# Attention and feed-forward on one core: the opening's order on all five engines as lists of numbers

## The chip, the cores and the metric

The kernel runs on one core of a Trainium2 chip. The metric is the device time of one execution in microseconds (us). TensorE (PE), VectorE (DVE), ScalarE (ACT), GpSimd (POOL) and SyncE (SP, which here issues nearly all DMAs) each work through a list of their own, in order, and wait for one another by semaphores.

## The reference, cut to what matters

Eight batches, eight heads of 64 columns, 512 local and 32 global tokens. Local tokens attend to a band of 32 positions on both sides and to the global tokens; global tokens attend to everything. What comes out, 8 x 544 rows of 512, goes through a feed-forward layer with a residual:

```python
xn = (x - mu) / np.sqrt(var + 1e-06) * g_ln
ch = np.maximum(xn @ w_ch1, 0.0) @ w_ch2      # 512 -> 2048 -> 512
return (x + ch).astype(np.float32)
```

## The kernel before, in words

**Chunks and units.** The local rows are cut into eight chunks of 512 rows (one batch, two halves of 256 rows), the global rows form a ninth. Attention is done in units: one pair of heads of one half. A unit has `score` (32 PE matmuls), four `lowest` (DVE), four `exp` (ACT), `turn` (4 PE transposes) and `turned` (ACT copy), `sums` (32 PE matmuls), `total` (POOL), `inverse` and `scale` (DVE). The first chunk has units 0 to 7, four for each half. After a half's four units come `stats`, `join`, `widen` (DVE), `root` (POOL) and `apply` (DVE, one of the four on ACT), which norm the rows, and then the turning of the normed rows: `turn_x` on PE, `high_x` on ACT and `low_x` on DVE, which split a float32 into two terms for PE.

**Feed-forward.** Each chunk runs through 16 weight blocks f: `first` (three groups of four 128x512 matmuls into `ph`), `high` (ACT, `hh`, L694) and `low` (DVE, `hl`, L698), and `second` (three matmuls for each of four row tiles). The next block's `first` reuses the one bank of `ph`, so it waits for the `hl` before it. Below, FFN0 and FFN1 are the `first` of blocks 0 and 1 in the first chunk, and hh0, hl0, hl1, ... the two terms of a block's result.

**Weights.** Each block is loaded once in a packed form (`raw`, two DMAs, .0 for the first matrix and .1 for the second) and unpacked during the first chunk, in two parts of seven steps: `size`, `third` and `high` on ACT (L293, L296, L315), `bound`, `place`, `sign` and `low` on DVE (L300, L303, L309, L319). Four places hold raw blocks, so block 4 can be loaded when block 0's `sign` steps are done, and so on.

**Later units.** While a chunk is in its feed-forward, PE visits the next chunk's units two at a time: a *visit* scores two units and sums the two before them. Units 8 to 15 are visited in the first chunk.

**The planner.** No order is left to the framework. `begin_plan` describes every operation to `Plan.op` (engine, cost, key, what it comes after), numbered here from 0 as they are described, and `Plan.emit` plays the engines in a model: among an engine's operations that can start soonest (within `PATIENCE`) it takes the smallest key, emits it and adds its cost to the engine's time. The model also has the DMA wire, and PE's code, fetched in pages of 256 words while PE works (`PAGE`, `FETCH`). In PE's idle time it emits dummy matmuls (`none`, L810).

Of the kernel before, what the change touches and what calls it, by code (L numbers as in the profile page):

```python
# [75 lines left out]
IN_FLIGHT = 8  # L76
STORING = 6


class Plan:  # L80


# [6 lines left out]
    def op(self, engine, cost, key, run, *after, behind=None, late=0.0, size=0.0, words=8):  # L89
        o = Operation(engine, cost, key, run, after, behind, late, size)  # L90
        o.words = words
        self.waiting[engine].append(o)
        self.count += 1
        return o

    def emit(self):
# [11 lines left out]
        wire, landed, paused = FIRST_BYTE, [], False  # L108
        words, fetched = 0, 0.0
        while self.count:  # L110
# [12 lines left out]
            o = can[e].pop(n)[1]  # L123
            self.count -= 1
            o.end = t + o.cost * (COLD[1] if e == "PE" and t < COLD[0] else 1.0)
            if e == "PE":
                spare = SPARE * (COLD[1] if t < COLD[0] else 1.0)
                idle = max(free[e], AWAKE)
                for _ in range(int((t - idle - MARGIN) / spare) if t < FULL else 0):
                    words += 2 * self.spare(idle)  # L130
                for n in range(words, words + o.words):
                    if n % PAGE == PAGE_AT and t < FULL:
                        now = t + o.cost * (n - words) / o.words
                        if n > PAGE:
# [25 lines left out]
class Operation:  # L160
    def __init__(self, engine, cost, key, run, after, behind, late, size):
        self.engine, self.cost, self.key, self.run = engine, cost, key, run
        self.after = flat(after)
        self.behind, self.late, self.size, self.end = behind, late, size, None

    def lands(self):
        return self.end + self.late + LATENCY

    def ready(self):
        t = self.behind.end if self.behind else 0.0  # L170
        for a in self.after:
            same = a.engine == self.engine and not a.size
            t = max(t, a.end if same else a.end + a.late + LATENCY)
        return t

@with_exitstack
def attention_ffn_kernel(
# [185 lines left out]

    xtags = cycle(["x0", "x1", "x2"])

    def new_x():
        return fpool.tile([P, 2, DM], F32, name="x", tag=next(xtags))

# [417 lines left out]
    def begin_plan(plan):  # L786
# [45 lines left out]
        for n, u in enumerate(us):  # L832
# [8 lines left out]
            for c in range(4):  # L841
# [11 lines left out]
            turned[n] = op(  # L853
                *(("DVE", 0.69) if n in ON_DVE else ("ACT", 0.57)), key + 0.4,
                lambda u=u, n=n: u.turned(n in ON_DVE), turn[n], sums.get(n - 2)
# [14 lines left out]
            def stats(u=u, it=it, hp=hp, j=0):  # L870
                if hp == j == 0:
                    it["norm"] = Norm(u.x, range(2), HP)
                it["norm"].stats(j, hp)
# [6 lines left out]
            if hp < HP - 1:  # L880
# [6 lines left out]
            join = [  # L887
                op("DVE", 0.17, key, lambda it=it, j=j: it["norm"].join(j), it["stats"])
                for j in range(2)
# [4 lines left out]
            for j in range(2):  # L894
                on_act = 2 * half + j in APPLY_ACT

                def apply_to(it=it, j=j, half=half, on_act=on_act):
                    if "to" not in it:
                        it["to"] = new_x() if half else wpool.tile([P, 2, DM], F32, name="x", tag="w4")
# [4 lines left out]
                apply.append(op(  # L904
                    *(("ACT", 0.81) if on_act else ("DVE", 0.55)), key, apply_to, root,
                    it["shift"] if on_act else [],
# [18 lines left out]
            def split_in(k2, it=it, half=half, key=key):  # L925
                for kt in (2 * k2, 2 * k2 + 1):
# [10 lines left out]
                    it["high"].append(op("ACT", 0.38, key + 0.2, high_half, it[k2, "t"], g,  # L937
                                         it["high"][-1:]))
                    it["low"].append(op("DVE", 0.41, key + 0.3, low_half, it["high"][kt]))
# [8 lines left out]
        xl = half_of[1]["low"]  # L948
        xh = half_of[1]["high"]

# [4 lines left out]
        for f in range(NF):  # L955
# [17 lines left out]
            for part, c in enumerate(  # L973
# [3 lines left out]
                key += W2_LATE * part  # L977
                size = op("ACT", 1.13 if wide else 0.6, key, lambda s=s, c=c: s.size(c), raws[f][part if not wide else 1],
                          before)
                before = size  # L980
                third = op("ACT", 1.13 if wide else 0.6, key + 0.1, lambda s=s, c=c: s.third(c), size)
                on, cost = ("POOL", 1.15 if wide else 0.65) if f in ON_POOL else ("DVE", 0.69 if wide else 0.36)
                bound = op(on, cost, key + 0.2, lambda s=s, c=c: s.bound(c), size)
                place = op("DVE", 1.22 if wide else 0.63, key + 0.3, lambda s=s, c=c: s.place(c), bound, third)
                sign[f].append(op("DVE", 1.22 if wide else 0.63, key + 0.4, lambda s=s, c=c: s.sign(c), place))
                high[f].append(op("ACT", 1.04 if wide else 0.56, key + 0.5, lambda s=s, c=c: s.high(c), sign[f][-1]))
                on, cost = ("POOL", 2.3 if wide else 1.2) if f in ON_POOL else ("DVE", 1.22 if wide else 0.63)
                low[f].append(op(on, cost, key + 0.6, lambda s=s, c=c: s.low(c), high[f][-1]))


# [23 lines left out]
        def visit(key, us, prev, nxt):  # L1014
# [31 lines left out]
            for j, u in enumerate(us):  # L1046
# [18 lines left out]
                t = op("POOL", 0.23, key + 0.3, lambda u=u: u.total(), exps)  # L1065
                inverse_of[u] = op("DVE", 0.17, key + 1.0, lambda u=u: u.inverse(), t)
                if not locals_:
# [6 lines left out]
                    for k in range(16):  # L1074
                        turned_of[u].append(
                            op("DVE", 0.31, key + 2, lambda u=u, k=k: u.transposes(*divmod(k, 4)),
                               turned_of[u][1:])
# [7 lines left out]
                else:  # L1085
                    o = []
                    for k in range(16):
                        o.append(op("DVE", 0.31, key + SLACK, lambda u=u, k=k: u.transposes(*divmod(k, 4)),
                                    exps, o[-1:], v))
# [6 lines left out]
            for u in prev:  # L1096
                banks[2].append(op("DVE", 0.42, key + 0.1, lambda u=u: u.scale(), v, inverse_of[u]))
                if u.at[1] == HP - 1:
# [4 lines left out]
        def finish(u, key, scales):  # L1103
# [17 lines left out]
            for j in js:  # L1121
                st.append(op("DVE", 0.69, key, lambda j=j: stats(j), scales, st[-1:]))
            join = [op("DVE", 0.17, key, lambda j=j: it["norm"].join(j), st) for j in js]
            widen = op("DVE", 0.14, key, lambda: it["norm"].widen(), join)
# [46 lines left out]
        for c, chunk in enumerate(chunks):  # L1171
# [29 lines left out]
            for f in range(NF + 1):  # L1201
                key = nominal(c, f)
                if f < NF:
# [26 lines left out]
                    if 2 * f in beside:  # L1230
                        beside[2 * f].behind = end
                    hh[c, f] = op("ACT", 0.59 if wide else 0.38, key - URGENT, lambda f=f, box=box: box[0].high(f),
                                  end, second.get((c, f - 2, nt - 1)))
                    hl[c, f] = op("DVE", 0.66 if wide else 0.39, key - URGENT, lambda f=f, box=box: box[0].low(f),
                                  hh[c, f])
# [179 lines left out]
```

## Time and profile before

| | us |
|---|---|
| median of 3 runs | 908.24 (905.89 to 909.13) |
| the profiled execution, whole | 908.04 |
| its span, first to last instruction | 906.3 |
| PE busy in the span | 890.3 |
| DVE busy | 692.0 |
| ACT busy | 311.5 |
| first feed-forward matmul starts | 39.96 |
| start from which PE has no gap until the end | 45.13 |

A time in the rows is counted from the span's first instruction. A timeline line gives the start, the duration (of a group: from the first to the last), engine, line, operation, tile and, in brackets, the idle time of the engine before it and what ended that. `pv` is what `sums` writes, `sc` what `score` writes, `tp` what `turn` writes, `t` what `turn_x` writes, `x` what `scale` and `apply` write. "issue" as a releaser means that the engine waited for nothing that the profile shows.

### The profile page before, as it was taken

What the parts mean: (1) busy time and instruction counts of PE and PEld (TensorE: products, weight loads), DVE (VectorE), ACT (ScalarE), POOL (GpSimd) and SP (SyncE); (2) the same over time, 40 slices, a digit from 0 to 9 for tenths busy, and PEclk for the clock granted to TensorE, in tenths of its full rate; (3) what the DMA queues carried; (4) which work ended last, traced back from release to release, by engine and by line L of the source; (5) the groups of instructions that cost most, each with busy time, mean ns of one, the idle gap of its engine ahead of it and who ended that gap; (6) DMA issues with size and microseconds to landing.
All of it is one profiled execution on the core that took longest, in us unless ns stands there. A gap on an engine that the chain in (4) does not pass through costs nothing.

```text
span 906.3 us, 21438 instructions
## 1 busy us (share of the span) xinstructions
PE 890.3 (98%) x8523; PEld 709.3 (78%) x8523; DVE 692.0 (76%) x2432; ACT 311.5 (34%) x881; POOL 39.8 (4%) x133
## 2 busy tenths in 40 slices
PE   6899999999999999999999999999999999999997
PEld 4488878888788888878888887888888877777896
DVE  4999998798878888788878896888876266766411
ACT  6799863223223223323323222322323122222211
POOL 4101000000000000000000000000000000000000
PEclk9999999999999999999999999999999999999999
DMA  9787654324124313324332403332331435455200
GB/s 352 278 314 248 227 172 146 100 80 148 37 93 141 111 70 125 102 77 148 105 99 99 148 3 122 108 120 100 125 102 53 155 123 216 156 180 204 67 17 24
DMA packets 42868, 119.88 MB, mean 132 GB/s; under 512 B 5136, under 2 KB 7184, under 8 KB 40720
## 3 DMA queue, kind: packets, MB, share of 16 engines
q1 hardware_dynamic: 42576, 118.25, 37.2%
q8 instruction: 67, 1.10, 0.5%
q14 instruction: 33, 0.27, 0.1%
q10 hardware_dynamic: 192, 0.26, 0.1%
HBM read 100.67 MB, written 17.83 MB: 131 GB/s over the span
## 4 chain that ended last, share of the span: by engine, by line
PE 94%; DVE 0%; issue 0%
PE ph L685 42%; PE acc L710 42%; PE sc L405 3%; PE pv L460 3%; PE pv L594 1%; PE sc L519 1%; PE t L645 0%; PE tp L441 0%; PE tp L567 0%; PE pv L530 0%; DVE tmp L303 0%; DVE ob L722 0%; DVE hl L698 0%
## 5 line engine op out<-in xcount | busy, mean ns | idle before, releaser
L710 PE MATMUL acc<-w,hh 128*128 128x512 f32 x1088 | 342.3, 396 | 0.0
L685 PE MATMUL ph<-xh,w 128*128 128x512 f32 (+1 forms) x1216 | 308.5, 380 | 1.2 <-DVE hl L698 1.0
L685 PEld LDWEIGHTS ph<-xh,w 128*128 128x128 f32 x1216 | 215.7, 188 | 49.4 <-DVE hl L698 1.7
L710 PEld LDWEIGHTS acc<-w,hh 128*128 128x128 f32 x1088 | 205.3, 189 | 47.3
L694 ACT ACTIVATE hh<-ph 128x512 fp32r<-128x512 f32 (+1 forms) x144 | 82.5, 573 | 429.9 <-PE ph L685 400.2
L710 PE MATMUL acc<-w,hl 128*128 128x512 f32 x544 | 218.5, 402 | 0.0
L452 DVE STREAM_TRANSPOSE pt<-p 32x128 f32<-32x128 f32 x768 | 206.1, 289 | 9.4 <-ACT p L429 1.0
L698 DVE SCALAR_TENSOR_TENSOR hl<-ph,hh 128x512 fp32r<-128x512 f32 (+1 forms) x144 | 95.2, 661 | 123.9 <-ACT hh L694 123.1
L685 PE MATMUL ph<-xl,w 128*128 128x512 f32 x512 | 141.2, 397 | 0.0
L429 ACT ACTIVATE p<-p,mn 128x128 f32<-128x128 f32 x256 | 99.6, 392 | 91.2 <-DVE mn L417 91.2
L710 PEld LDWEIGHTS acc<-w,hl 128*128 128x128 f32 x544 | 102.2, 188 | 23.2
L685 PEld LDWEIGHTS ph<-xl,w 128*128 128x128 f32 x512 | 95.8, 188 | 23.6
L653 DVE STREAM_TRANSPOSE tmp<-x 32x128 f32<-32x128 f32 x320 | 96.7, 302 | 4.8
L417 DVE CUSTOM_DVE_ANT_0 p<-sc,mask 128x128 f32<-128x128 f32 x256 | 59.2, 284 | 22.7 <-PE sc L405 20.9
L429 ACT ACTIVATION_READ_ACCUMULATOR p<-p,mn 128x1 f32 x256 | 48.4, 189 | 0.0
L472 POOL TENSOR_SCALAR ri<-sm 128x4 f32<-128x4 f32 x64 | 16.7, 262 | 628.8 <-ACT p L429 627.3
L577 DVE STREAM_TRANSPOSE gpt<-gp 32x128 f32<-32x128 f32 x128 | 38.6, 302 | 2.0
L479 DVE TENSOR_TENSOR x<-pv,ri 128x256 f32<-128x256 f32 x64 | 24.5, 419 | 13.4 <-PE pv L460 13.4
L405 PEld LDWEIGHTS sc<-u_e 64*32 64x32 f32 x1792 | 24.9, 106 | 10.2 <-issue 9.5
L405 PE MATMUL sc<-u_e 64*32 64x128 f32 x1792 | 32.4, 274 | 0.0
L460 PE MATMUL pv<-u_v,pt 128*32 128x64 f32 x1792 | 30.8, 221 | 0.0
L460 PEld LDWEIGHTS pv<-u_v,pt 128*32 128x32 f32 x1792 | 26.3, 110 | 5.7 <-issue 5.7
(71 smaller groups left out, 505.1 us busy)
## 6 DMA issues: line engine op xcount, KB each, us to landing
u_v<-in_ev SPq DMA_DIRECT2D x56, 512.0 KB, 4.8
u_e<-in_eq SPq DMA_DIRECT2D x56, 336.0 KB, 6.3
raw<-in_wd SPq DMA_DIRECT2D x32, 512.0 KB, 7.0
gk<-in_gk SPq DMA_DIRECT2D x8, 1152.0 KB, 6.6
xs<-x SPq DMA_DIRECT2D x32, 256.0 KB, 6.0
ob<-xs SPq DMA_DIRECT2D x32, 256.0 KB, 5.1
out<-ob SPq DMA_DIRECT2D x32, 256.0 KB, 3.5
gv<-in_gv SPq DMA_DIRECT2D x8, 1024.0 KB, 4.9
```

Source lines behind the costliest of these rows:

```text
L405: nc.tensor.matmul(sc[h][gp, qb * P:(qb + 1) * P], self.e[hd, w * WIN:(w + 1) * WIN], self.e[hd, k0 * WIN:(k0 + 4) * WIN], start=True, sto ...
L417: nc.vector.tensor_tensor_reduce(out=self.p[:, c], in0=self.sc[h][:, qb * P:(qb + 1) * P], in1=masks[self.at[2], qb], scale=-QSCALE, scala ...
L429: nc.scalar.activation(self.p[:, c], self.p[:, c], AF.Exp, bias=self.mn[:, c:c + 1], scale=-1.0, accum_out=self.sm[:, c:c + 1],)
L452: nc.vector.transpose(out=self.pt[rp, :, gp], in_=self.p[gp, :, rp])
L460: nc.tensor.matmul(pv[gp, qb * P + h * D:qb * P + h * D + D], self.pt[:, 2 * h + qb, gp], self.v[:, 4 * qb + g, h * D:(h + 1) * D], start= ...
L479: nc.vector.tensor_tensor(self.x[:, :, hp * P:(hp + 1) * P].rearrange("p q (h d) -> p q h d", h=2), self.pv[:, :256].rearrange("p (q h d) ...
L577: nc.vector.transpose(out=self.pt[rp, 0, :, ip], in_=p[ip, :, r])
L653: nc.vector.transpose(out=dst[rp, 2 * half:2 * half + 2, :, i], in_=src[ip, :, k:k + 2, r])
L685: nc.tensor.matmul(self.ph[f][:, :self.n], w[:, kt, :], xx[kt][:, :self.n], start=begins and kt == 0, stop=ends and kt == KT - 1,)
L694: nc.scalar.activation(hh[:, :self.n], self.ph[f][:, :self.n], AF.Relu)
L698: nc.vector.scalar_tensor_tensor(hl[:, :self.n], self.ph[f][:, :self.n], 0.0, f32(hh[:, :self.n]), ALU.max, ALU.subtract,)
L710: nc.tensor.matmul(self.acc[t], a[:, ts], w, start=(f == 0 and i == 0), stop=(f == NF - 1 and i == 2),)
```

## The change

Until its list is used up, an engine takes the operation whose number its list gives next, and no key counts; then the keys take over again. The lists hold the first chunk and some operations of the second: 26 numbers for POOL, 91 for SP, 174 for PE, 227 for ACT, 358 for DVE.

```diff
+        order = {}
+        for e, text in ORDER.items():
...
             for e, ops in can.items():
+                if order[e]:
+                    ops = [(t, o) if o.number == order[e][-1] else (1e9, o) for t, o in ops]
+                    if all(t == 1e9 for t, _ in ops):
+                        continue
                 if not ops:
...
             o = can[e].pop(n)[1]
+            if order[e]:
+                order[e].pop()
```

The stretch of the lists that matters here, in the names above (s unit n as n; W f.p is part p of weight block f; h0, h1 the two halves of the rows):

```
PE   score 0 1 2, turn0, score3, turn1, score4, sums0, turn2, score5, sums1, turn3, score6, sums2,
     turn4, sums3, score7, turn5, sums4, turn6, sums5, turn7, sums6, turn_x h0 (two), sums7,
     turn_x h0 (two), turn_x h1 (four), FFN0, visit 0, FFN1, second of block 0, ...
DVE  ... scale3, three stats, join, lowest7.0, join, widen, lowest7.1, lowest7.2, scale4, lowest7.3,
     stats, W0.1 place, shift, apply0 h0, inverse5, scale5, three stats, inverse7, W0.1 sign,
     inverse6, scale6, W1.0 bound, two stats, low_x h0, scale7, two stats, two joins, widen,
     low_x h0, W1.0 place, W0.0 low, apply h1 (two), low_x h0 (two), W1.0 sign, low_x h1 (four),
     W0.1 low, W1.1 bound, place, sign, W1.0 low, hl0, W1.1 low, ...
ACT  ... exp7.0, turned5, exp7.3, exp7.1, exp7.2, turned6, apply1 h0, W1.0 size, turned7, high_x h0,
     W1.0 third, high_x h0, W1.1 size, W0.0 high, W0.1 high, high_x h0 (two), high_x h1 (four),
     W1.1 third, W1.0 high, W2.0 size, W2.0 third, W2.1 size, hh0, W1.1 high, ..., hh1, ...,
     hh3, W6.0 size, W6.1 size, exp, W6.1 third, exp, exp, W5.0 high, exp, hh4, ...
SP   eq of units 0 1 2 4, raw0.0, eq3, eq5, ev0, eq6, ev2, ev1, raw0.1, raw1.0, ev3, g, eq7, ev4, ev5,
     ev6, raw1.1, raw2.0, ev7, raw2.1, raw3.0, raw3.1, eq8, raw4.0, raw4.1, eq9, eq11, eq10, a store,
     raw5.0, ev8, raw5.1, a store, ev9, ev10, raw6.0, a store, raw6.1, eq13, raw7.0, ...
```

(`eq` and `ev` are the two loads of a unit, scores' and sums' operands.) Besides the lists, the model's costs are set anew (for example 0.36 with a drain of 0.09 for `bound`, 1.22 to 1.14 for a whole `place`, 0.17 to 0.1 for `inverse`, 0.66 to 0.605 for `hl`, 0.31 to 0.275 for a 32x32 transpose), and these hold for all chunks:

```diff
-            inverse[n] = op("DVE", 0.17, key + 0.6, lambda u=u: u.inverse(), total[n])
-            scale[n] = op("DVE", 0.42, key + 0.6, lambda u=u: u.scale(), sums[n], inverse[n])
+            inverse[n] = op("DVE", 0.1, key + 0.6, lambda u=u: u.inverse(), total[n])
+            scale[n] = op("DVE", 0.34, key + 0.6, lambda u=u: u.scale(), sums[n], inverse[n])
+            inverse[n].drain = scale[n].drain = DRAIN
...
-                    hl[c, f] = op("DVE", 0.66 if wide else 0.39, key - URGENT, lambda f=f, box=box: box[0].low(f),
+                    hl[c, f] = op("DVE", 0.605 if wide else 0.34, key - URGENT, lambda f=f, box=box: box[0].low(f),
```

And some dependencies are now written down so that any order keeps them: `high_x` of h1 comes after that of h0, FFN0 after `low_x` of both halves, the second chunk's first `scale` after the last reading of the row tile that it overwrites (`x_read`), and the row tile for h1's normed rows is named ("x2") where it was the next in a cycle. No operation is added or taken away, but the number of dummy matmuls follows the model's idle time.

## Rows read from the trace of the kernel before

**Rows 1.** The chain of waits that ended last, in order of time: start, duration, what. One block's `second`, twelve matmuls as in a `first`.
```profile
48.20 2.81 PE acc L710 x12
```

**Rows 2.** Busy time of each engine in two stretches, with granted clock, DMA share and GB/s.
```profile
0.00:45.13 45.13, 33.91 (x656) 21.09 (x656) 30.54 (x133) 31.77 (x100) 11.76 (x52) 0.92 0.85 315
45.13:900.00 854.87, 854.87 (x7863) 687.29 (x7864) 660.05 (x2298) 279.69 (x781) 28.04 (x81) 1.00 0.35 123
```

**Rows 3.** Waits of PE in the whole span: who waited for whom, us in total, times, longest.
```profile
PE pv L460 <- issue: 4.8, 3, 2.3
...
PE pv L460 <- ACT pt L446: 1.3, 1, 1.3
...
PE ph L685 <- DVE hl L698: 1.0, 1, 1.0
```

**Rows 4.** PE's timeline where the two waits for "issue" end and where as many instructions again have gone by; then the busy time of each engine (PE, PEld, DVE, ACT, POOL, with their instructions) between those points, with PE's granted clock, the DMA share and GB/s.
```profile
14.87 0.53 PE L460 MATMUL pv<-u,pt 128*32 128x64 f32 x19 [2.30 <-issue]
...
20.90 1.07 PE L460 MATMUL pv<-u,pt 128*32 128x64 f32 x28 [2.27 <-issue]
...
26.03 1.17 PE L460 MATMUL pv<-u,pt 128*32 128x64 f32 x32
...
14.86:20.89 6.03, 3.75 (x127) 2.66 (x127) 3.70 (x25) 4.44 (x20) 0.44 (x2) 0.95 1.03 412
20.89:26.95 6.06, 6.05 (x132) 4.67 (x131) 3.61 (x18) 2.64 (x8) 0.94 (x2) 0.50 1.02 412
```

**Rows 5.** Busy time of each engine in the microsecond in which PE's clock is back, columns as in rows 4.
```profile
27.00:28.00 1.00, 0.79 (x25) 0.46 (x22) 0.71 (x3) 1.00 (x5) 0.00 (x0) 0.97 1.02 418
```

**Rows 6.** PE's timeline from the last unit's turn to the end of the last gap.
```profile
28.64 0.72 PE L441 MATMUL tp<-ident,p 128*128 128x128 f32 x4
...
32.16 0.65 PE L460 MATMUL pv<-u,pt 128*32 128x64 f32 x32 [1.29 <-ACT pt L446]
...
37.19 1.11 PE L645 MATMUL t<-ident,x 128*128 128x128 f32 x8
...
39.96 1.18 PE L685 MATMUL ph<-xh,w 128*128 128x512 f32 x4
...
42.94 1.16 PE L405 MATMUL sc<-u_e 64*32 64x128 f32 x64
45.13 1.21 PE L685 MATMUL ph<-xh,w 128*128 128x512 f32 x4 [1.04 <-DVE hl L698]
```

**Rows 7.** DVE's timeline: the last `lowest` of the opening, the end of unit 7 and the second half's norm, the last `low_x`, and the steps before hl0. The last line is from DVE's groups by line and shape up to 45.13 us: busy time, mean ns of one | idle time before them.
```profile
28.11 0.27 DVE L417 CUSTOM_DVE_ANT_0 p<-sc,mask 128x128 f32<-128x128 f32 x1
...
33.52 0.42 DVE L479 TENSOR_TENSOR x<-pv,ri 128x256 f32<-128x256 f32 x1
33.98 0.49 DVE L331 BATCH_NORM_STATS2 st<-x 128x6 f32<-128x128 f32 x2
34.38 0.38 DVE L334 BATCH_NORM_AGGREGATE mv<-st 128x2 f32<-128x24 f32 x2
...
36.59 1.00 DVE L356 TENSOR_SCALAR x<-x,mv,rs 128x512 f32<-128x512 f32 x2
...
39.31 1.65 DVE L663 SCALAR_TENSOR_TENSOR xl<-t,g_sb,xh 128x256 fp32r<-128x256 f32 x4
...
41.93 0.69 DVE L303 SCALAR_TENSOR_TENSOR tmp<-tmp,raw 128x512 int32<-128x512 int32 x1
42.66 0.69 DVE L309 SCALAR_TENSOR_TENSOR tmp<-raw,tmp 128x512 int32<-128x512 int32 x1
43.27 0.42 DVE L300 TENSOR_SCALAR tmp<-tmp 128x512 f32<-128x512 f32 x1
43.78 0.70 DVE L303 SCALAR_TENSOR_TENSOR tmp<-tmp,raw 128x512 int32<-128x512 int32 x1
44.39 0.69 DVE L698 SCALAR_TENSOR_TENSOR hl<-ph,hh 128x512 fp32r<-128x512 f32 x1
...
L417 DVE CUSTOM_DVE_ANT_0 p<-sc,mask 128x128 f32<-128x128 f32 x32 | 7.5, 282 | 6.9 <-PE sc L405 5.4 <-ACT tmp L293 0.7 <-POOL mask L251 0.5
```

**Rows 8.** ACT's timeline: the opening's last `exp` and what follows it, the copy of unit 7's turn, the last `high_x`, and hh0.
```profile
28.49 0.39 ACT L429 ACTIVATE p<-p,mn 128x128 f32<-128x128 f32 x1
...
28.88 0.67 ACT L293 ACTIVATE tmp<-raw 128x512 f32<-128x512 f32 x1
29.45 0.66 ACT L296 ACTIVATE raw<-raw 128x512 int32<-128x512 uint16 x1
...
31.53 0.58 ACT L446 COPY pt<-tp 128x512 f32<-128x512 f32 x1
...
38.12 1.57 ACT L659 ACTIVATE xh<-t,g_sb 128x256 fp32r<-128x256 f32 x4 [1.91 <-PE t L645]
...
43.04 0.60 ACT L694 ACTIVATE hh<-ph 128x512 fp32r<-128x512 f32 x1 [0.60 <-PE ph L685]
```

**Rows 9.** POOL's timeline: the second half's `root`.
```profile
35.05 1.09 POOL L341 TENSOR_TENSOR rs<-rs,neg_half 128x2 f32<-128x2 f32 x1 [5.44 <-DVE rs L337]
```

**Rows 10.** SP's issues of blocks 6 and 7 and of the next unit's operands; then the landing times of the raw tiles issued from 45 to 75 us.
```profile
48.61 9.39 SPq L264 DMA_DIRECT2D raw<-in_wd  x4
58.52 0.80 SPq L264 DMA_DIRECT2D u_v<-in_ev  x2
...
DMA to landing us min/median/max: 4.3/6.2/9.0
```

More of the change, by code (lines that the diff above doesn't have):

```diff
@@ L1 @@
 from contextlib import ExitStack
-from itertools import cycle
+from itertools import chain as run_on, cycle
 import concourse.bass as bass
@@ L91, in op @@
         o.words = words
+        o.number = self.count
         self.waiting[engine].append(o)
@@ L109, in emit @@
         words, fetched = 0, 0.0
+        order = {}
+        for e, text in ORDER.items():
+            order[e] = []
+            for run in text.split():
+                a, _, b = run.partition("-")
+                order[e] += range(int(a), int(b or a) + 1)
+            order[e].reverse()
         while self.count:
@@ L164, in __init__ @@
         self.behind, self.late, self.size, self.end = behind, late, size, None
+        self.drain = 0.0
     def lands(self):
@@ L172, in ready @@
             same = a.engine == self.engine and not a.size
-            t = max(t, a.end if same else a.end + a.late + LATENCY)
+            t = max(t, a.end + a.drain if same else a.end + a.late + LATENCY)
         return t
@@ L362, in att, with new_x @@
         return ps_a.tile([P, 512], F32, name=name, tag=f"att{k}")
-    xtags = cycle(["x0", "x1", "x2"])
-    def new_x():
-        return fpool.tile([P, 2, DM], F32, name="x", tag=next(xtags))
+    xtags = run_on(["x0", "x1"], cycle(["x0", "x1", "x2"]))
+    def new_x(tag=None):
+        return fpool.tile([P, 2, DM], F32, name="x", tag=tag or next(xtags))
     class Local:
@@ L853, in begin_plan @@
             turned[n] = op(
-                *(("DVE", 0.69) if n in ON_DVE else ("ACT", 0.57)), key + 0.4,
+                *(("DVE", 0.69) if n in ON_DVE else ("ACT", 0.48)), key + 0.4,
                 lambda u=u, n=n: u.turned(n in ON_DVE), turn[n], sums.get(n - 2)
@@ L870, in stats @@
             def stats(u=u, it=it, hp=hp, j=0):
-                if hp == j == 0:
+                if "norm" not in it:
                     it["norm"] = Norm(u.x, range(2), HP)
@@ L887, in begin_plan @@
             join = [
-                op("DVE", 0.17, key, lambda it=it, j=j: it["norm"].join(j), it["stats"])
+                op("DVE", 0.1, key, lambda it=it, j=j: it["norm"].join(j), it["stats"])
                 for j in range(2)
@@ L898, in apply_to @@
                     if "to" not in it:
-                        it["to"] = new_x() if half else wpool.tile([P, 2, DM], F32, name="x", tag="w4")
+                        it["to"] = new_x("x2") if half else wpool.tile([P, 2, DM], F32, name="x", tag="w4")
                     (it["norm"].apply if on_act else it["norm"].apply_to)(j, it["to"])
@@ L904, in begin_plan @@
                 apply.append(op(
-                    *(("ACT", 0.81) if on_act else ("DVE", 0.55)), key, apply_to, root,
+                    *(("ACT", 0.72) if on_act else ("DVE", 0.46)), key, apply_to, root,
                     it["shift"] if on_act else [],
@@ L935, in low_half @@
                         low_x(it[kt], *(a[:, cols] for a in xt[kt]), kt)
-                    it["high"].append(op("ACT", 0.38, key + 0.2, high_half, it[k2, "t"], g,
-                                         it["high"][-1:]))
-                    it["low"].append(op("DVE", 0.41, key + 0.3, low_half, it["high"][kt]))
+                    it["high"].append(op("ACT", 0.36, key + 0.2, high_half, it[k2, "t"], g,
+                                         it["high"][-1:], half_of[0]["high"][kt:kt + 1] if half else []))
+                    it["low"].append(op("DVE", 0.395, key + 0.3, low_half, it["high"][kt]))
             steps = [(k2, j) for k2 in range(2) for j in range(2)]
@@ L947, in begin_plan @@
                     split_in(k2)
-        xl = half_of[1]["low"]
-        xh = half_of[1]["high"]
+        xl = half_of[0]["low"] + half_of[1]["low"]
+        xh = half_of[0]["high"] + half_of[1]["high"]
         step = 6.7
@@ L977, in begin_plan @@
                 key += W2_LATE * part
-                size = op("ACT", 1.13 if wide else 0.6, key, lambda s=s, c=c: s.size(c), raws[f][part if not wide else 1],
+                size = op("ACT", 1.11 if wide else 0.575, key, lambda s=s, c=c: s.size(c), raws[f][part if not wide else 1],
                           before)
                 before = size
-                third = op("ACT", 1.13 if wide else 0.6, key + 0.1, lambda s=s, c=c: s.third(c), size)
-                on, cost = ("POOL", 1.15 if wide else 0.65) if f in ON_POOL else ("DVE", 0.69 if wide else 0.36)
+                third = op("ACT", 1.11 if wide else 0.575, key + 0.1, lambda s=s, c=c: s.third(c), size)
+                on, cost = ("POOL", 1.15 if wide else 0.65) if f in ON_POOL else ("DVE", 0.64 if wide else 0.36)
                 bound = op(on, cost, key + 0.2, lambda s=s, c=c: s.bound(c), size)
[L984 to L987, printed above, removed]
+                bound.drain = DRAIN
+                place = op("DVE", 1.14 if wide else 0.605, key + 0.3, lambda s=s, c=c: s.place(c), bound, third)
+                place.drain = DRAIN
+                sign[f].append(op("DVE", 1.14 if wide else 0.605, key + 0.4, lambda s=s, c=c: s.sign(c), place))
+                high[f].append(op("ACT", 1.0 if wide else 0.53, key + 0.5, lambda s=s, c=c: s.high(c), sign[f][-1]))
+                on, cost = ("POOL", 2.3 if wide else 1.2) if f in ON_POOL else ("DVE", 1.14 if wide else 0.605)
                 low[f].append(op(on, cost, key + 0.6, lambda s=s, c=c: s.low(c), high[f][-1]))
+        x_read = [half_of[k]["apply"] + half_of[k]["stores"] for k in range(2)] + [half_of[1]["turn"]]
         free = [[turned[n0 - 2]], [turned[n0 - 1]], lowest[n0 - 1]]
@@ L1065, in visit @@
                 t = op("POOL", 0.23, key + 0.3, lambda u=u: u.total(), exps)
-                inverse_of[u] = op("DVE", 0.17, key + 1.0, lambda u=u: u.inverse(), t)
+                inverse_of[u] = op("DVE", 0.1, key + 1.0, lambda u=u: u.inverse(), t)
                 if not locals_:
@@ L1075, in visit @@
                         turned_of[u].append(
-                            op("DVE", 0.31, key + 2, lambda u=u, k=k: u.transposes(*divmod(k, 4)),
+                            op("DVE", 0.275, key + 2, lambda u=u, k=k: u.transposes(*divmod(k, 4)),
                                turned_of[u][1:])
@@ L1087, in visit @@
                     for k in range(16):
-                        o.append(op("DVE", 0.31, key + SLACK, lambda u=u, k=k: u.transposes(*divmod(k, 4)),
+                        o.append(op("DVE", 0.275, key + SLACK, lambda u=u, k=k: u.transposes(*divmod(k, 4)),
                                     exps, o[-1:], v))
@@ L1096, in visit @@
             for u in prev:
-                banks[2].append(op("DVE", 0.42, key + 0.1, lambda u=u: u.scale(), v, inverse_of[u]))
+                read = x_read.pop(0) if u.at[1] == 0 and x_read else []
+                banks[2].append(op("DVE", 0.34, key + 0.1, lambda u=u: u.scale(), v, inverse_of[u], read))
                 if u.at[1] == HP - 1:
@@ L1121, in finish @@
             for j in js:
-                st.append(op("DVE", 0.69, key, lambda j=j: stats(j), scales, st[-1:]))
-            join = [op("DVE", 0.17, key, lambda j=j: it["norm"].join(j), st) for j in js]
+                st.append(op("DVE", 0.6, key, lambda j=j: stats(j), scales, st[-1:]))
+            join = [op("DVE", 0.1, key, lambda j=j: it["norm"].join(j), st) for j in js]
             widen = op("DVE", 0.14, key, lambda: it["norm"].widen(), join)
@@ L1231, in begin_plan @@
                         beside[2 * f].behind = end
-                    hh[c, f] = op("ACT", 0.59 if wide else 0.38, key - URGENT, lambda f=f, box=box: box[0].high(f),
+                    hh[c, f] = op("ACT", 0.5 if wide else 0.3, key - URGENT, lambda f=f, box=box: box[0].high(f),
                                   end, second.get((c, f - 2, nt - 1)))
-                    hl[c, f] = op("DVE", 0.66 if wide else 0.39, key - URGENT, lambda f=f, box=box: box[0].low(f),
+                    hl[c, f] = op("DVE", 0.605 if wide else 0.34, key - URGENT, lambda f=f, box=box: box[0].low(f),
                                   hh[c, f])
```

48 lines of the change are left out of this document (47 added, 1 removed).

## The prediction

> **What bounds the kernel now.** I looked first at the busy time of each engine, cut where PE's last gap ends. From 45.13 to 900 us PE is busy 854.87 of 854.87 us at full clock, while DVE has 195 us to spare [rows 2]: in that stretch an order can take nothing away, only break something. Before 45.13 PE is busy 33.91 us, so 11.22 us stand open at most, apart from the dummy matmuls in the busy part. So the end of the kernel is the time at which PE's unbroken run starts, plus a constant. The waits of PE came second [rows 3]: 4.8 us of "issue" (the engine waited for nothing that the profile shows), 1.3 us behind ACT's copy of a turn, 1.0 us behind hl0. PE's timeline shows where. Two waits of 2.30 and 2.27 us end at 14.87 and 20.90, with 127 matmuls and 127 weight loads between them, and the DMA engines are full all the while (share 1.03) [rows 4]. The planner has these in its model as PE's code, fetched in pages of 256 words; the row fits that, 254 instructions in 6.03 us. After the second wait the clock is at 0.50 (the 1.2 GHz level) until 26.95, during 6.05 us of PE work without a break, and back at 27 to 28 us [rows 4, 5].
>
> Then comes the chain that sets the start of the run [rows 6 to 8]. Unit 7's last `lowest` stands late in DVE's order, at 28.11, so its last exp is at 28.49 and its turn at 28.64; ACT copies that turn only at 31.53, behind weight steps and `high_x`; sums7 ends at 32.16 + 0.65 = 32.81; scale7 33.52, norm, two `apply` until 37.59, `turn_x`, `high_x`, FFN0 at 39.96, hl0 at 44.39 (hh0 was there at 43.64, DVE was at weight steps), FFN1 at 45.13.
>
> **The change part by part. Up to 20.90: nothing won, I say.** Both orders of PE have the same words in front of the two page borders but for which unit they are of, and the second page can't be asked for before the first border. The order puts raw0.0 and three more score operands ahead of ev0, so it lands as the eighth load: six of 0.344 MB and two of 0.524 (the tiles' sizes), 3.11 MB, some 7.5 us of wire at the 412 GB/s of [rows 4]. By estimate sums0 comes near 11.5, about 1 us later than now. Until 14.87 PE then has sums0, turn2 and part of score5 to do, some 2 us of work: the page wait covers it. If ev0 took 2 us longer, that cover is gone and everything behind moves by what is over; I keep 1 us for it. What DVE does in the wait is W0.0's steps (0.51 + 0.73 + 0.61 us [rows 7]) instead of nothing.
>
> **From 20.90 to sums5: same time.** The new order has the rest of sums3 (28 matmuls), score7 32, turn5 4, sums4 32, turn6 4, sums5 32: 132, as many as now between the same points [rows 4]. So sums5 ends near 26.03 + 1.17 = 27.2 in both, if the clock falls again (the wait in front is as long).
>
> **From sums5 to sums7: 2.15 us earlier.** score7 is one place earlier, and DVE's list has unit 7's four `lowest` behind scale3 and scale4, not behind scale5. sums4 ends near 25.2, scale4 takes 0.46 [rows 7], so lowest7.3 ends at 26.0 (0.23 each, 7.5 us for 32 [rows 7]); three exps at 0.39 [rows 8] end at 27.2, when turn7's place in PE comes: 27.25 to 27.9 against 28.64. Now DVE is the pace. From 26.0: stats 0.2, place 0.73, shift 0.1, apply 0.5, inverse 0.1, then scale5 from 27.6 to 28.05; three stats 0.6, inverse 0.1, sign 0.61, inverse with its drain 0.15, scale6 from 29.5 to 29.95 [durations: rows 7]. sums7 waits for scale6 (one bank) and for turned7. ACT reaches that in 0.58 + 0.8 + 0.57 + 0.58 us from 27.2, at 29.7 (two copies and a size by rows 8, `apply` 0.8 by estimate from DVE's 0.5 and the ratio of the two engines' steps), with no `high_x` ahead of it. sums7: 30.0 to 30.65, against 32.81.
>
> **From sums7 to FFN0: 0.4 us more.** DVE: bound 0.4, two stats 0.4 and a `low_x` 0.4 lie beside sums7 and run to 31.15; scale7 0.46, two stats 0.4, joins and widen 0.5 end at 32.5. `root` takes 1.09 on POOL [rows 9], but DVE's list puts `low_x`, place and low there, 0.39 + 0.7 + 0.61, so the two `apply` start at 34.15 and end at 35.1 (1.00 for both [rows 7]); now 37.59. From the applies' end to FFN0 the same steps follow as now, 39.96 - 37.59 = 2.37 us [rows 6, 7], with ACT free for `high_x`: FFN0 at 37.45. Dummy matmuls in front of `turn_x` may cost some tenths, as the model has to guess PE's idle time.
>
> **From FFN0 to FFN1: 0.75 us more.** FFN0 takes 42.94 - 39.96 = 2.98 us, so hh0 runs from 40.5 to 41.1 [rows 6, 8]. DVE from 35.1: two `low_x` 0.78, sign 0.61, four `low_x` 1.57, low 0.61, bound 0.51, place 0.73, sign 0.61, low 0.61 [rows 7]: 41.1, just in time. hl0 to FFN1 is 45.13 - 44.39 = 0.74 [rows 6, 7]: FFN1 at 41.85. Visit 0 covers all but 0.3 us of that wait; 1.0 us of it is there now.
>
> **Behind FFN1.** The same weight steps are due 3.3 us earlier. When hl0 is done DVE has behind it four bounds, places and signs and three lows; now it is five, five, four and three: 1.1 us less done. Summing DVE's list by the durations of rows 7 and 9, hl1 is done 5.2 us behind hl0 and wanted after 5.6 (a `first` and a `second`, 2.8 each [rows 1]); for the later blocks 1.5 to 5 us are left over. So I put no wait there, with hl1 as the thin spot. The new costs and `x_read` for later chunks add no work; PE's full 854.87 us and DVE's 195 us of slack [rows 2] hide another order, and I take 0 (at most a wait on one hl, some tenths).
>
> **Sum.** 45.13 - 41.85 = 3.3 us off the profiled execution's 908.04 (span 906.3): 904.75. The median shown lies 0.2 above that execution; I say 904.8.
>
> **A rule against the row.** By rows 4 PE twice stood 2.3 us at a border of 256 instructions. The Trainium skill (Runtime: NRT & Kernel Launch, section Instruction fetch mechanics) says that the sequencer fetches the next page while it executes the current one and that a border's cost is "mostly hidden". The trace disagrees while the DMA engines are full; by that rule the two waits could go with any order, and the first rival is what this would make.
>
> **Rivals.** *A page wait goes.* Were the second one shortened by its whole 2.27 us, sums3 would run at 18.6 to 19 and the clock would not fall: 904.75 - 2.27 = 902.5. For it: DVE's first 45 us hold 14.6 us of idle time [rows 2], so the rest could follow. Against: the instructions between the borders and the full DMA engines stay as they are. Chance 0.11.
>
> *Part is given back in the first chunk.* hl1 has 0.4 us to spare, hl4 about as little (below), ev0's load may land late (1 us), a dummy too many 0.4: with 1 to 3 us lost, 905.8 to 907.8, say 906.8. For it: everything is packed closer, and a late step now holds up the whole list behind it. Chance 0.21.
>
> *Slower: block 6's weights come late.* SP now issues the raw tiles of blocks 6 and 7 from 48.61 on and unit 10's ev at 58.52 [rows 10], when visit 1 has freed its buffer. The new list has ev10 in front of raw6.0 and raw6.1, and SP is in order, so they wait for visit 1: 58.52 - 45.13 = 13.4 us behind FFN1, so ev10 at 55.2 and raw6.1 near 56.4, while the run is 3.3 us earlier. It lands 4.3, 6.2 or 9.0 us later [rows 10]: 60.7, 62.6, 65.4. On ACT size W6.1 stands ahead of hh4, with four exps, a third and a high between: 0.57 + 2.65, then hh4 0.6 and hl4 0.74, hl4 done at 65.3, 67.2 or 70.0. FFN5 wants it at 41.85 + 25.5 = 67.3 (eight runs of 2.8 [rows 1]; visit 1 and two turns 3.1, an estimate from rows 6: 1.1 for two scores, 0.6 for each sums, 0.4 for each turn). With the shortest and the median landing nothing is lost; with the longest 2.7 us, and a PE idle that long may cost the clock: 6.05 us at half clock [rows 4] are 3.0 us lost. 904.75 + 2.7 + 3.0 = 910.4. It decides from a landing of 8.5 us on, where the idle time comes near the 2.3 us of rows 4; below that it is the case before. Chance 0.1.
>
> That the lists name other operations than meant is no rival: 657 to 661 fall on FFN0, hh0 and hl0 on three engines.
>
> **Chances and range.** Forecast 0.58, page wait 0.11, given back 0.21, slower 0.1. The forecast's own range is 903.7 to 905.8. To leave out half of the first rival and most of the last: 902.7 to 908.3. About 0.5% (4.5 us) is what a measurement of this kernel can tell from no change, so faster means under 903.7 and slower over 912.8: faster 0.13 (the first rival and the forecast's edge), slower 0.04 (a slower case with a second wait), within 0.83.
>
> **What would show it.** Right: two page waits again near 14.9 and 20.9; sums7 near 30.6; copy of turn7 before 30; FFN0 near 37.4; FFN1 near 41.8 with a gap of some 0.3 us in front; no gap of PE after that. Wrong: a page wait that is gone or moved; a gap of PE before FFN2 or FFN5 with hl or raw as the releaser; a clock of 0.50 anywhere after FFN0; a longer distance from FFN1 to the end than 906.3 - 45.13.

## The result, and the profile after

The changed kernel takes 913.81 us (median of 6 runs, 910.80 to 915.77) against 907.9 us for the kernel before: 1.0076 times as long, interval 1.0059 to 1.0093. I had said 904.8 us, and at most 908.3. The profiled execution took 915.23 us with a span of 913.4, 7.1 us more than the span before. The kernel before, e1 and e9 each had one disturbed execution, much longer than the others; it moves a median by less than 0.4 us and is in no ratio, no interval and no profile that is read here.

First the busy time of each engine, cut where the opening ends, which is now 42.80 us (columns as in [rows 2]).

```profile
0.00:42.80 42.80, 32.64 (x650) 20.45 (x650) 29.02 (x131) 31.87 (x100) 11.59 (x52) 0.96 0.80 303
42.80:900.00 857.20, 853.07 (x7821) 680.41 (x7822) 666.32 (x2297) 280.15 (x779) 28.98 (x81) 1.00 0.36 124
```

The opening is 2.33 us shorter than in [rows 2]: the change does there what it is meant to. But the second stretch, in which PE had no idle time before, now has 4.1 us of it, although it begins at full clock and its work is the same. The waits of PE and of its weight loads (PEld) say for whom:

```profile
PE pv L523 <- issue: 2.9, 2, 1.8
PE sc L468 <- DMA u_e<-in_eq: 2.0, 1, 2.0
...
PE ph L748 <- DVE hl L761: 1.6, 2, 1.3
...
PEld ph L748 <- DVE hl L761: 7.6, 15, 1.7
```

Against [rows 3], "issue" has fallen from 4.8 to 2.9 and the copy of the turn has left the head of the list. New are one wait of 2.0 us for a unit's `eq` in a visit (`u_e`), one of 1.3 for an `hl`, and 15 waits of weight loads for an `hl` (2 before, 1.7 us in all). PE's timeline has the places:

```profile
10.35 1.23 PE L468 MATMUL sc<-u 64*32 64x128 f32 x32 [1.16 <-DMA u<-in_eq]
...
16.19 0.63 PE L468 MATMUL sc<-u 64*32 64x128 f32 x20 [0.36 <-issue]
...
22.30 1.08 PE L523 MATMUL pv<-u,pt 128*32 128x64 f32 x30 [1.81 <-issue]
...
28.32 0.32 PE L523 MATMUL pv<-u,pt 128*32 128x64 f32 x7 [1.14 <-issue]
...
31.08 0.65 PE L523 MATMUL pv<-u,pt 128*32 128x64 f32 x32 [0.62 <-ACT xh L722]
...
38.32 1.18 PE L748 MATMUL ph<-xh,w 128*128 128x512 f32 x4
...
42.80 1.20 PE L748 MATMUL ph<-xh,w 128*128 128x512 f32 x4 [0.34 <-DVE hl L761]
...
69.94 0.73 PE L748 MATMUL ph<-xh,w 128*128 128x512 f32 x2 [1.29 <-DVE hl L761]
...
99.50 0.67 PE L468 MATMUL sc<-u_e 64*32 64x128 f32 x32 [2.05 <-DMA u_e<-in_eq]
100.11 1.71 PE L523 MATMUL pv<-u_v,pt 128*32 128x64 f32 x64
101.75 2.08 PE L748 MATMUL ph<-xh,w 128*128 128x512 f32 x4
```

The lines marked "issue" answer to [rows 4], the three after them to [rows 6]: sums7 at 31.08 (32.16 before), FFN0 at 38.32 (39.96), FFN1 at 42.80 (45.13). Then come two gaps that the kernel before does not have. The second costs more than its 2.05 us, as the busy time by microsecond shows (seventh column: PE's granted clock):

```profile
100.00:101.00 1.00, 1.00 (x60) 0.90 (x48) 0.74 (x7) 0.13 (x1) 0.00 (x0) 0.71 0.84 233
101.00:102.00 1.00, 1.00 (x33) 0.83 (x26) 1.00 (x2) 1.00 (x4) 0.00 (x0) 0.50 0.83 250
...
104.00:105.00 1.00, 1.00 (x6) 0.82 (x5) 0.36 (x1) 0.00 (x0) 0.00 (x0) 1.00 0.99 377
```

At the half clock (0.50, the 1.2 GHz level) the sums of the visit and the `first` behind it take 5.47 us, from 100.11 to 105.58; in e4 below, at full clock, the same work takes 3.93. So the half clock costs some 1.5 us.

Last, the length of a later chunk. Each has one double `second`, 24 matmuls in a row, and the chain of waits shows its start. First two of the kernel before, 395.73 us and four chunks apart, then three lines of the changed kernel:

```profile
240.30 5.61 PE acc L710 x24
...
636.03 5.61 PE acc L710 x24
```

```profile
235.78 3.07 PE ph L748 x12
...
244.67 5.62 PE acc L773 x24
...
642.34 5.61 PE acc L773 x24
```

A chunk takes (642.34 - 244.67) / 4 = 99.42 us where it took 395.73 / 4 = 98.93, and a `first` that took 2.80 us before takes 3.07 at 235.78. So the 7.1 us are made up of: opening -2.33; from FFN1 to the first of these marks 201.87 instead of 195.17, +6.70; the four chunks up to the last mark +1.94; from there to the end 271.06 instead of 270.27, +0.79. Of the 6.70, 3.34 are the two gaps and 1.5 the half clock; 0.5 fit the second chunk, if it lengthens like the others. Of the rest, about 1.3, some 0.85 lie at the end of the first chunk: from the `first` before the normed rows are turned to the `first` behind the next visit the changed kernel takes 16.04 us (139.68 to 155.72), the kernel before 15.19 (136.63 to 151.82). Three weight loads wait there, 0.58 and 0.29 us for an `hl` and 0.45 for a `low_x`, on DVE's work. The last 0.4 to 0.5 us were not found.

### The profile page after: what moved, and what is told of

Its sections match the earlier page's. It is cut to its first block, busy times and chain, and to the rows that moved or that the text cites. A ratio compares the mean times of both kernels' runs of the same rounds, so it can differ in the third digit from the quotient of the medians.

```text
span 913.4 us, 21426 instructions
## 1 busy us (share of the span) xinstructions
PE 894.3 (98%) x8517; PEld 708.0 (78%) x8517; DVE 698.0 (76%) x2432; ACT 313.2 (34%) x881; POOL 40.6 (4%) x133
## 4 chain that ended last, share of the span: by engine, by line
PE 85%; DVE 2%; DMA 2%; SPq 0%; issue 0%; ACT 0%; DVEq 0%; ACTq 0%
PE ph L748 38%; PE acc L773 38%; PE pv L523 3%; PE sc L468 3%; PE pv L657 1%; DMA u_e<-in_eq 1%; DVE pt L515 1%; DMA gk<-in_gk 1%; PE sc L582 1%; SPq L327 0%; PE tp L630 0%; PE t L708 0%; DVE ob L785 0%; DVE xl L726 0%; DVE w L382 0%
## 5 line engine op out<-in xcount | busy, mean ns | idle before, releaser
L515 DVE STREAM_TRANSPOSE pt<-p 32x128 f32<-32x128 f32 x768 | 214.9, 293 | 10.3 <-ACT p L492 1.1
```

The source lines that it names most:

```text
L515: nc.vector.transpose(out=self.pt[rp, :, gp], in_=self.p[gp, :, rp])
```

## The experiments

**The two gaps: what stands in SP's list.** SP's timeline of the changed kernel (start, duration until the last of the issues in the line has gone out, what is loaded or stored):

```profile
45.68 10.81 SPq L327 DMA_DIRECT2D u_v<-in_ev  x2
56.60 0.37 SPq L327 DMA_DIRECT2D raw<-in_wd  x1
...
57.49 0.42 SPq L327 DMA_DIRECT2D raw<-in_wd  x1
...
80.36 1.37 SPq L327 DMA_DIRECT2D u_v<-in_ev  x1
87.17 0.33 SPq L327 DMA_DIRECT2D xs<-x  x1
...
90.08 0.65 SPq L327 DMA_DIRECT2D u_e<-in_eq  x1
```

The first line is ev9 and ev10; ev10 goes out only at the line's end, when visit 1 has freed its buffer, and raw6.0 and raw6.1 go out behind it at 56.60 and 57.49. ACT's timeline shows when the second was there, and the step that hl4 needs:

```profile
65.39 0.66 ACT L356 ACTIVATE tmp<-raw 128x512 f32<-128x512 f32 x1 [2.39 <-DMA raw<-in_wd]
...
68.59 0.57 ACT L757 ACTIVATE hh<-ph 128x512 fp32r<-128x512 f32 x1
```

The later gap has the same form: from 81.7 to 87.17 SP issues nothing, because a store stands next that waits for the `scale` of unit 10, which DVE has from 86.73 to 87.13. Behind the store stand raw10.1 and the last loads of units 14 and 15. eq15 goes out at 90.08, and the score of unit 15 gets it at 99.50. Two kernels move one number each:

```diff
-480 508 292 176 293 511 308
+480 292 176 293 508 511 308
```

(e4: ev10, 508, behind raw6.1, 293)

> One number moved in SP's list: ev10 (508), which waits for visit 1, stands behind raw6.1 (293). Theory A (raw6 waits on SP behind ev10, so ACT's size stands 2.4 us and hh4, hl4 and FFN5 come late): the gap in front of FFN5 (1.29 us and some tenths in the weight loads) is gone, the time falls by 1 to 2 us if nothing else is short. Rival (DVE has too much to do in the first chunk, and the gap only moves): a gap of about the same size in front of FFN6 or a later block.

```diff
-540 545 357 372 539
-541 373 542 388-389
+540 357 372 539
+541 373 542 545 388-389
```

(e3: the store, 545, behind eq15, 542)

> One number moved in SP's list: the first store of the half that unit 11 ends (545) stands behind raw11.1 and in front of eq15's neighbour, not in front of raw10.1. Theory A (SP stands at that store until DVE's late scale of unit 10, so eq15 is issued only some 7 us before its need and lands too late): the wait of PE's score for eq (2.05 us) is gone, and the half-speed clock behind it too, the time falls by 2 to 4 us. Rival (the DMA wire is full there and eq15 lands late wherever SP issues it): the wait stays over 1 us.

SP in e4 (raw6.0, then ev10), then in e3 (eq15):

```profile
51.97 0.33 SPq L327 DMA_DIRECT2D raw<-in_wd  x1
...
56.30 0.33 SPq L327 DMA_DIRECT2D u_v<-in_ev  x1
```

```profile
87.30 0.67 SPq L327 DMA_DIRECT2D u_e<-in_eq  x1
```

Measured: e4 909.99 us, 1.0023 times before [1.0013, 1.0033]; e3 911.36, 1.0037 [1.0025, 1.0049]. In e4 raw6.0 goes out 4.6 us earlier, with an opening as long (FFN1 at 42.92), and the gap before FFN5 is gone. It takes most of the other gap with it: with visit 1 and all behind it earlier, the store goes out at 84.64 and eq15 at 88.05, and 0.23 us of the 2.05 are left. In e3 the gap for eq15 is gone and that before FFN5 stays, 1.17 us. So each number is shown to be the cause of its gap, and the two losses are not additive. The landings were slow as well (raw6.1 7.9 us after its issue and 5.6 in e4; eq15 9.4, and 6.9 in e3), but that follows the order too.

**The chunks: which of the new costs.** The new costs hold for all chunks, the lists for the first alone. One kernel has the costs without the lists, the others give costs back one at a time, or put one into the kernel before.

```diff
-ORDER = {
...
-}
+ORDER = {e: "" for e in ("PE", "DVE", "ACT", "POOL", "SP")}
```

> All lists empty, so the keys order everything again; new costs and dependencies stay. Theory A: FFN1 starts near 45 us as before the change, no gap of 1.3 or 2.05 us in the first chunk, but the later chunks take 99.4 us: span some 3 to 4 us over the 906.3 of the kernel before, 909 to 911. Rival (what makes the later chunks long is the order that the lists leave behind, not the costs): later chunks 98.9, span near 906.

e2: 913.67 us, 1.0062 [1.0039, 1.0085]. A chunk is 99.40 us, FFN1 starts at 45.49, and there is one gap, 1.29 us for an `hl` at 121.44. So the costs by themselves make the kernel as slow as the whole change does; the lists win the opening's 2 to 3 us and lose them again in the two gaps.

```diff
-op("DVE", 0.275, key + 2, lambda u=u, k=k: u.transposes(*divmod(k, 4)),
+op("DVE", 0.31, key + 2, lambda u=u, k=k: u.transposes(*divmod(k, 4)),
```

(e1, in the changed kernel; the same at a second place, with `key + SLACK`)

> The lists as changed, but the model's cost of a 32x32 transpose put back from 0.275 to 0.31 (both places); all other new costs stay. Theory A (the chunks behind the first are longer because the model now packs more transposes in front of an hl than fit): the later chunks return from 99.42 to about 98.93 us each, the waits of PE's weight loads for hl (7.6 us, 15 times in the changed kernel) fall to about those of the first chunk (under 3.5 us), the time falls by 3 to 3.5 us. Rival (the new costs of hh and hl, or x_read, do it): chunks stay at 99.4 and the time within 1 us. The two gaps of the first chunk (1.29 and 2.05 us) stay in either case.

e1: 910.64 us, 1.0030 [1.0013, 1.0047]. A chunk is back at 98.92, and both gaps are still there (1.55 and 2.11 us). So the planned cost of a 32x32 transpose, taken back by itself in the changed kernel, takes back the chunks' loss.

```diff
-op("DVE", 0.31, key + 2, lambda u=u, k=k: u.transposes(*divmod(k, 4)),
+op("DVE", 0.275, key + 2, lambda u=u, k=k: u.transposes(*divmod(k, 4)),
```

(e9, and e11 for a second look, in the kernel before, at both places)

> The kernel before, with the cost of a 32x32 transpose at 0.275 in place of 0.31 and nothing else. Theory A: the opening as before, later chunks 99.4 us in place of 98.9, span 909 to 911. Rival (it takes the other new costs with it to make the chunks longer): chunks 98.9 and the time within 1 us of the kernel before.

> The kernel before with the transposes planned at 0.275 instead of 0.31, once more, for the length of a chunk, which its first profile does not give. Its list has 20, 18 and 17 transposes in front of single `hl`. Theory A: a later chunk is 99.4 us; as its time was that of before, the opening must then have won about as much as the chunks lost. If a chunk is 98.9, the transposes' cost does nothing by itself, and the length comes only with another of the new costs.

e9: 907.19 us, 1.0000 [0.9985, 1.0014]; e11: 1.0001 [0.9984, 1.0019], a chunk 98.92 us. So that cost by itself does nothing to the kernel before, which speaks against the simple theory. The costs of `hh` and `hl` were the next suspects:

```diff
-hh[c, f] = op("ACT", 0.5 if wide else 0.3, key - URGENT, lambda f=f, box=box: box[0].high(f),
+hh[c, f] = op("ACT", 0.59 if wide else 0.38, key - URGENT, lambda f=f, box=box: box[0].high(f),
-hl[c, f] = op("DVE", 0.605 if wide else 0.34, key - URGENT, lambda f=f, box=box: box[0].low(f),
+hl[c, f] = op("DVE", 0.66 if wide else 0.39, key - URGENT, lambda f=f, box=box: box[0].low(f),
```

(e6: in the changed kernel; e10: the reverse, in the kernel before)

> The changed kernel with the planner's old costs of `high` and `low` in a block (ACT 0.59 and 0.38, DVE 0.66 and 0.39); the transposes stay at the new 0.275. Theory A (a transpose planned at 0.275 lets the planner put up to 18 or 19 of them in front of one `hl`, where the kernel before had 16 in a row; the list of this kernel has 18 and 19 too): a later chunk stays at 99.4 us, PEld waits for `hl` stay near 7 us, FFN1 to the end stays near 869. Theory B (the cheaper `hh` and `hl` are what brings the late ones): a later chunk is 98.9 and the distance some 2.5 us less. The two gaps behind FFN1 (1.2 and 2.0 us) stay in both.

> The kernel before with only the new costs of `high` and `low` in a block (ACT 0.5 and 0.3, DVE 0.605 and 0.34). Its list keeps 16 transposes in front of nearly every `hl`, with one group of 18 in a chunk, as before. Theory A (transposes): a later chunk stays at 98.9 us and the time within 0.15% of before. Theory B (`hh`, `hl`): a later chunk is 99.4 us, the time some 2.5 us more.

e6: 911.69 us, 1.0033 [1.0018, 1.0047], with the two gaps (1.88 and 2.20 us) and a chunk of 99.09, between the two theories. e10: 907.97, 1.0006 [0.9993, 1.0019], a chunk 98.91. So neither cost by itself makes the chunks of the kernel before longer. DVE's timeline tells why, in the changed kernel and then in e11, at the same place of a chunk:

```profile
421.34 0.69 DVE L761 SCALAR_TENSOR_TENSOR hl<-ph,hh 128x512 fp32r<-128x512 f32 x1 [0.38 <-ACT hh L757]
422.06 5.67 DVE L515 STREAM_TRANSPOSE pt<-p 32x128 f32<-32x128 f32 x18
427.76 0.69 DVE L761 SCALAR_TENSOR_TENSOR hl<-ph,hh 128x512 fp32r<-128x512 f32 x1
428.48 1.58 DVE L515 STREAM_TRANSPOSE pt<-p 32x128 f32<-32x128 f32 x5
430.08 3.78 DVE L716 STREAM_TRANSPOSE tmp<-x 32x128 f32<-32x128 f32 x12
...
434.61 5.07 DVE L716 STREAM_TRANSPOSE tmp<-x 32x128 f32<-32x128 f32 x16
439.71 0.69 DVE L761 SCALAR_TENSOR_TENSOR hl<-ph,hh 128x512 fp32r<-128x512 f32 x1
```

```profile
416.86 0.69 DVE L698 SCALAR_TENSOR_TENSOR hl<-ph,hh 128x512 fp32r<-128x512 f32 x1 [1.27 <-ACT hh L694]
417.58 4.69 DVE L452 STREAM_TRANSPOSE pt<-p 32x128 f32<-32x128 f32 x18
422.46 0.69 DVE L698 SCALAR_TENSOR_TENSOR hl<-ph,hh 128x512 fp32r<-128x512 f32 x1 [0.19 <-ACT hh L694]
...
434.16 0.69 DVE L698 SCALAR_TENSOR_TENSOR hl<-ph,hh 128x512 fp32r<-128x512 f32 x1
```

Between the four `hl` the changed kernel has 18 + 17 + 16 = 51 transposes and no idle time: DVE is the bound there, for 439.71 - 421.34 = 18.37 us. The first and the last of the same four `hl` in e6 and in e1:

```profile
420.86 0.69 DVE L761 SCALAR_TENSOR_TENSOR hl<-ph,hh 128x512 fp32r<-128x512 f32 x1
...
438.91 0.69 DVE L761 SCALAR_TENSOR_TENSOR hl<-ph,hh 128x512 fp32r<-128x512 f32 x1
```

```profile
420.92 0.69 DVE L761 SCALAR_TENSOR_TENSOR hl<-ph,hh 128x512 fp32r<-128x512 f32 x1
...
438.33 0.69 DVE L761 SCALAR_TENSOR_TENSOR hl<-ph,hh 128x512 fp32r<-128x512 f32 x1
```

e6 has 18 + 16 + 16 = 50 transposes there and takes 18.05 us, e1 has 16 + 16 + 16 = 48 and takes 17.41. The chunks are longer by 0.49, 0.17 and 0.00 us: what is over 17.88 in each case (18.37 - 0.49 = 18.05 - 0.17 = 17.88), so that is about what PE leaves DVE. e2 bears it out: 51 transposes, 18.38 us, a chunk longer by 0.47. One transpose fewer, 0.315 us, is 0.33 us of the chunk. e11 has 18 + 17 + 16 as well, but its 18 `pt` took 0.26 us each and not 0.315; it takes 17.30 and its chunk loses nothing. So the cause is a sum: what the planner puts between the `hl`, which the costs of transposes and of `hh` and `hl` set together, and the pace of a transpose, which has two values: at this place 0.315 in e1, e2, e6 and the changed kernel and 0.26 in the kernel before, e10 and e11.

The pace goes with the order. Two units share this stretch of DVE's list and take turns, sixteen transposes each, numbered k = 0 to 15. The planner, played through for each kernel and laid beside its trace, gives the unit and the k of every transpose. Where the two units are in step (k of one, then the same k of the other), the second starts 0.236 us after the first and the next 0.274 us after that. Where one unit is a step ahead, every transpose starts 0.316 us after the one before. This holds wherever three of them follow without a break, in the twelve kernels with an undisturbed profile (all but e9), 70 to 213 times for each kind of step in each: the two short steps are never over 0.28 us, the long ones never under 0.31. At the place above, the changed kernel has one unit a step ahead and e11 has the two in step. So the pace is the planner's doing too, and that is how the kernel before could be planned with 0.275 and lose nothing. No run changes this step alone, and which of the new costs puts one unit ahead was not found (it is not the transposes' own: in e1 the unit is still ahead).

**The opening: eq3 first.** Score3 now waits 1.16 us for its operand, which SP issues behind raw0.0 and eq4. e5 puts it ahead:

```diff
-0 2 4 8 196 6 10 1 12
+0 2 4 6 8 196 10 1 12
```

> The changed kernel with eq3 ahead of eq4 and raw0.0 in SP's list, nothing else. Theory B: the first page border, the third border and FFN1 0.5 to 1.3 us earlier than in the changed kernel (16.19, 28.32, 42.80). Rival: no difference beyond that between runs.

e5: 915.14 us in one execution, FFN1 at 43.12: not earlier. The score no longer waits, but the sums behind it wait 1.79 us for their `ev`.

**All together.** e7 has the edits of e1, e3 and e4, e8 that of e5 as well.

> The three repairs together: transposes at 0.31, the store behind eq15, ev10 behind raw6.1. Theory A (three separate losses that add up): no gap over 0.5 us behind FFN1, later chunks 98.9 us, FFN1 somewhere in the 41.5 to 44.4 us that the runs so far showed, so a span of FFN1 + 861.2 (what the kernel before takes from there) = 902.7 to 905.6 and a median of 904.5 to 907.5: faster than before by 1 to 3 us. Rival (the losses hide one another, and a fourth one comes up where these go): a median of 908 or more.

> As e7_all, and in SP's list eq3 goes ahead of eq4 and raw0.0. Theory B (the opening is paced by score3's wait for eq3, 1.0 to 1.5 us, which moves the first page border and with it the second and third, 6 us apart): score3 starts by 9.7 us in place of 10.2 to 10.8, the page waits end about 1 us earlier, FFN1 comes 0.5 to 1.3 us earlier than in e7_all, and the median is 0.5 to 1.3 us lower. Rival (ACT and DVE set the opening, and raw0.0 that lands later stops ACT at the first size): FFN1 not earlier than in e7_all.

e7: 906.98 us, 0.9992 [0.9981, 1.0004]; e8: 906.61, 0.9986 [0.9975, 0.9998]. In e7 FFN1 starts at 42.05 and the way from there to the end is 861.75 us (before: 906.3 - 45.13 = 861.17): with the three edits the loss behind FFN1 is gone but for 0.6 us, which settles that SP's two orders and the transposes' cost are what was lost. What is left fits the end of the first chunk, which takes 16.05 us here too (15.19 before). e8 is the one version with an interval below the kernel before, by 0.14%; from e7 it can't be told. Its fourth edit doesn't show in PE's timeline as the reason:

```profile
9.12 1.11 PE L468 MATMUL sc<-u 64*32 64x128 f32 x32
...
16.35 0.65 PE L523 MATMUL pv<-u,pt 128*32 128x64 f32 x32 [2.07 <-ACT p L492]
...
22.44 1.07 PE L523 MATMUL pv<-u,pt 128*32 128x64 f32 x30 [2.07 <-issue]
...
42.92 1.20 PE L748 MATMUL ph<-xh,w 128*128 128x512 f32 x4 [0.33 <-DVE hl L761]
```

Score3 (9.12) has no wait, but from 22.44 on everything stands where it stood: the page wait ends 0.14 us after that of the changed kernel, and FFN1 starts 0.12 us after.

## Why the prediction was wrong, step by step

- **Bound:** right for the kernel before, and taken too far. "An order can take nothing away, only break something" was my own sentence; then I looked for breaks at hl1 and hl4 only.
- **"Up to 20.90: nothing won":** wrong by 1.3 us. ev0 was not what came late: the borders ended at 16.19 and 22.30, behind a score3 that waited 1.16 us for eq3. A third page wait of 1.14 us, at 28.32, was in none of my steps. The three borders end 6.11 and 6.02 us apart, the two of the kernel before 6.03, and 5.9 to 6.5 in every run in which two borders in a row end in a wait. So in these rows, with the DMA engines full, a page wait is what PE's work leaves of some 6 us. Before, PE filled them at half clock, for 6.05 us without a break [rows 4]; the changed kernel was back at full clock from 25.4 on, was done sooner, and waited.
- **Sums5 to FFN1:** the mechanism was right and the steps almost to size. sums7 came 1.1 us after my time, the applies' end 0.85 (35.95), FFN0 0.87, FFN1 0.95: I put that down to the later borders, carried along. No run shortens a border by itself, but the eight profiled kernels with this order of PE's opening, sorted by the end of the third page wait (26.35 in e3 to 29.01 in e1), are sorted by FFN1 as well (41.52 to 44.42). Of the 3.3 us 2.33 came.
- **"Behind FFN1 I put no wait there":** this step failed, and it is the largest. hl1, my thin spot, held. What broke was SP's order, twice: 1.29 and 2.05 us of idle PE and 1.5 us of half clock. The first break is my slower rival: its chain (0.57 + 2.65 + 0.6 + 0.74 us from the raw tile's landing) gives 65.39 + 4.56 = 69.95, and FFN5 started at 69.94. Its size was 1.29 us, not 2.7, and no clock fell. I held it unlikely since I took the landing times of [rows 10] over, whose median is 6.2; with ten issues within 6 us behind ev10 the landing took 7.9 us from its issue at 57.49. The second break I never looked for: I followed SP's list to raw7.0 and no further, and the store ahead of eq15 stands eleven entries on. With the half clock it cost more than the first.
- **"The new costs for later chunks: I take 0":** failed too. "DVE's 195 us of slack" is a sum over the stretch; at the one place where 51 transposes stand between four `hl`, DVE has none. It cost 0.49 us in a later chunk and some 3 us in all; e1 takes back 3.2 (913.81 to 910.64).
- **Page rule:** the Trainium skill (Runtime: NRT & Kernel Launch, section Instruction fetch mechanics) calls a border's cost "mostly hidden". Here waits of 0.36, 1.81 and 1.14 us ended at the three borders, with the DMA engines full (share 1.01 to 1.03 in the stretches before them), so the trace still disagrees. The rival in which the second wait goes did not come true. The first wait nearly went, from 2.30 to 0.36, and that won nothing, as score3's wait for eq3 (1.16) stood in front of it.
- **A slip in the sum:** 904.75 + 0.2 is 904.95, and not 904.8. It changes nothing in the account.

## What to carry to other kernels

When a list fixes the order of a queue that is served in order, go through it to its end and ask of each entry that waits (a store for its result, a load for a free buffer) which loads stand behind it and when they are wanted: both gaps here were a load that needed nothing, behind an entry that waited. When costs of a planner are lowered, count what it then packs between two steps that the bound engine waits for; spare time summed over a stretch says nothing about that place, and the order in which two alike tasks alternate can change how long each takes. And a gain in an opening that hands the same work on earlier is kept only if what follows was not already just in time.

## What I had not expected of the hardware

Eighteen transposes on DVE, 32x128 floats each, at the same place of a chunk took 5.67 us in one kernel and 4.69 in another. What differs is whether the two units that take turns are in step or one step apart (above); it goes by groups of 32, the same in every later chunk but the last. Why the step matters to DVE, the traces don't show.

A wait of PE did not always cost it the clock. After 2.05 us the changed kernel fell to 0.50 for about 3 us, and e6 after 2.20; after 2.11 us e1 did not, nor e6 after 1.88 (a microsecond after each of these two waits, columns as above; e1, then e6):

```profile
103.00:104.00 1.00, 1.00 (x15) 0.81 (x5) 1.00 (x2) 1.00 (x4) 0.00 (x0) 1.00 0.73 262
```

```profile
70.00:71.00 1.00, 1.00 (x5) 0.82 (x5) 0.49 (x1) 1.00 (x4) 0.00 (x0) 1.00 1.01 404
```

And the opening is not of one length: with the same 573 matmuls in the same order up to FFN0, FFN1 started at 42.80 in the changed kernel, 41.52 in e3, 42.05 in e7 and 44.42 in e1, one profiled execution each. That is as much as the whole gain I had forecast.
